# A decode attention and MLP kernel: score and PV matmuls of 32 columns, PV in slices, and weights in other slots

## The chip, the cores and the metric

One core of one Trainium2 chip. The metric is the time on the device in microseconds (us). All runs told here were of the fast state (none over 1.5% above the quickest of the same kernel), each experiment was timed in the same rounds as the kernel before, and ratios are to that kernel. TensorE does the matmuls ("PV" below is the product of the softmax weights with V), VectorE and ScalarE copy and do the softmax, SyncE requests the transfers.

## The reference

Two layers of single-token attention over a long cache, each followed by an MLP block, for two sequences. Cut to what matters:

```python
# B, Sq, D = 2, 1, 576;  H, Sk, Dh = 32, 16384, 128;  F = 4608;  all bf16
def _A_ref(x, k_cache, v_cache, wq, wo):
    q = (x @ wq).reshape(B, Sq, H, Dh).transpose(0, 2, 1, 3)
    scores = jnp.einsum("bhqd,bhkd->bhqk", q, k_cache) * (Dh ** -0.5)
    p = _softmax(scores, axis=-1)
    o = jnp.einsum("bhqk,bhkd->bhqd", p, v_cache)
    return o.transpose(0, 2, 1, 3).reshape(B, Sq, H * Dh) @ wo

def _B_ref(x, w1, w2, w3, w4):          # with S = 1 the shifted parts of h vanish,
    ...                                 # so w1 and w2 add nothing to the result
    x1 = x + hs
    return x1 + _gelu(_layernorm(x1) @ w3) @ w4

x = A_x
for _ in range(2):
    x = x + _A_ref(_layernorm(x), A_k_cache, A_v_cache, A_wq, A_wo)
    x = x + _B_ref(_layernorm(x), B_w1, B_w2, B_w3, B_w4)
```

The K and V caches are read once per layer: 64 (sequence, head) pairs of 4.19 MB of K and 4.19 MB of V, twice. With the weights that is 1122 MB, far more than anything else the kernel does.

## The kernel before

A "head" below is one such pair: 16384 cache rows, that is 128 blocks of 128 rows for K and as many for V. K and V each have five slots in on-chip memory; a slot takes half a head (64 blocks, 2.097 MB), so a head needs four transfers. All are requested by SyncE, in order.

TensorE works in groups of 8 blocks: it transposes 8 K blocks into PSUM, VectorE or ScalarE copies them into `ktbuf`, and two groups later TensorE multiplies them by q, one column each:

```python
for gi, (u, gu, go) in enumerate(groups):          # 16 groups of a head
    if gi + LA < n_g:
        emit_transposes(*groups[gi + LA])          # LA = 2 groups ahead
    ...
    emit_evac(go)                                  # copy tps -> ktbuf, VectorE or ScalarE
    ...
    skey = emit_scores(i, u, gu, go, extra)
    if i >= 1:                                     # small softmax steps of the head before
        if gi == 3:    chain_stage2(hg - 1)
        elif gi == 7:  chain_stage3(hg - 1)
        elif gi == 11: chain_stage4(hg - 1)
state["go"] += n_g
chain_stage1(hg, skey)
if i >= 1:
    emit_pv(i - 1, hg - 1)                         # all 128 PV matmuls of the head before
```

```python
def emit_scores(i, u, gu, go, extra_waits):
    ...
    qcol = qT_sb[:, 2 * h + b:2 * h + b + 1]
    for jj in range(GRP):                          # GRP = 8
        ...
        pe.matmul(sps[:, pb, col:col + 1], ktbuf[:, w, jj * P128:(jj + 1) * P128], qcol, ...)

def emit_pv(i, hg):
    ...
    for half in range(NU):
        P.wait_dma("pe", sd_v[slot], vtot)
        for j in range(UB):                        # UB = 64
            pe.matmul(ops[:, col:col + 1], vslot(slot)[:, j * DH:(j + 1) * DH],
                      pbuf[:, pb, c:c + 1], start=fm, stop=lm)
```

The cache block is the stationary operand in both, so every matmul has its own weight load (16384 of each in both groups of the page). Each K request waits until the last transposes of its slot, each V request until the slot's PV matmuls:

```python
if gu == GPU - 1:                                  # in emit_transposes
    state["kslot_last_t"][slot] = (("tp", e), cnt)
    issue_k_upto(u + NSK)
```

The weights have no room of their own: `wq` and `w4` lie in V slots, `wo` and `w3` in K slots, and they wait until those are free:

```python
wq_sb = vreg[:, 0:DC * H * DH].rearrange("p (c n) -> p c n", c=DC)
wo_sb = kreg[:, 0:H * D].rearrange("p (h n) -> p h n", h=H)
...
if (not first) and u < NSK:
    waits.append(("m1", state["mlp1"]))            # K of layer 2 waits for the w3 product
...
load_wo([t for t in state["kslot_last_t"] if t is not None])   # after the last head
emit_pv(NH - 1, hg0 + NH - 1)
```

## Time and profile before

| | before |
|---|---|
| median of the first 3 runs | 2894.87 us (2872.96 to 2900.3) |
| span of the profiled run, mean granted clock | 2885.2 us, 0.753 |
| TensorE matmul and weight load busy | 83% and 79% |
| transfers | 1122.16 MB, 389 GB/s, 93.6% busy |

How such views are read. In the page's slices a digit is a tenth, and PEclk is the TensorE clock that was granted. In a stretch the columns are its bounds and length, the busy time of TensorE matmul, TensorE weight load, VectorE, ScalarE and GpSimd, then granted clock, DMA share and GB/s. A row of a group has busy time and mean length of one instruction in ns, then the idle time before them and what ended it. Matmul lengths are modelled and overlap; the distance between starts is the better measure of what one costs.

The page of the kernel before: the chain of work that ended last by engine, three groups of TensorE, and the loads of a K or V slot with their time to landing.

```profile
PE 72%; DVE 11%; issue 8%; DMA 5%; ACT 2%; SPq 2%; DVEq 0%; ACTq 0%
...
L415 PE MATMUL tps<-ident,kreg 128*128 128x128 bf16 x16384 | 1604.8, 257 | 57.6 <-issue 44.0
...
L451 PE MATMUL sps<-qT_sb,ktbuf 128*128 128x1 bf16 x16384 | 751.1, 167 | 253.6 <-DVE ktbuf L432 183.6
...
L539 PE MATMUL ops<-pbuf,vreg 128*128 128x1 bf16 x16384 | 449.0, 164 | 92.5 <-issue 86.2
...
kreg<-in_A_k_cache_dram SPq DMA_DIRECT2D x256, 2048.0 KB, 10.7
vreg<-in_A_v_cache_dram SPq DMA_DIRECT2D x256, 2048.0 KB, 17.6
```

The chain runs through TensorE for 72% of the span and through a transfer for 5%, although the transfers are 93.6% busy. The PV matmuls (L539) hardly wait for V: their idle time is "issue", time with no releaser. The scores (L451) wait for the copies of the transposed blocks.

### The profile page before, as it was taken

What the parts mean: (1) busy time and instruction counts of PE and PEld (TensorE: products, weight loads), DVE (VectorE), ACT (ScalarE), POOL (GpSimd) and SP (SyncE); (2) the same over time, 40 slices, a digit from 0 to 9 for tenths busy, and PEclk for the clock granted to TensorE, in tenths of its full rate; (3) what the DMA queues carried; (4) which work ended last, traced back from release to release, by engine and by line L of the source; (5) the groups of instructions that cost most, each with busy time, mean ns of one, the idle gap of its engine ahead of it and who ended that gap; (6) DMA issues with size and microseconds to landing.
All of it is one profiled execution on the core that took longest, in us unless ns stands there. A gap on an engine that the chain in (4) does not pass through costs nothing.

```text
span 2885.2 us, 108634 instructions
## 1 busy us (share of the span) xinstructions
PE 2396.5 (83%) x50814; PEld 2273.3 (79%) x50814; DVE 1121.5 (39%) x2626; ACT 787.8 (27%) x1084; POOL 1.3 (0%) x9
## 2 busy tenths in 40 slices
PE   6888898888888888887568887888988889888885
PEld 6788888888888788887357887888878788878883
DVE  3343433344443444334134434443343444334441
ACT  2222222223222223222023222222222322223220
POOL 0000000000000000000000000000000000000000
PEclk9777765688876887668678758877687886777776
DMA  9999999999999999998879999999999999999985
GB/s 393 414 375 421 401 388 378 376 413 416 422 409 378 403 410 425 402 381 350 309 294 425 414 380 396 410 404 407 406 391 397 421 417 391 400 374 402 408 342 214
DMA packets 95593, 1122.16 MB, mean 389 GB/s; under 512 B 8740, under 2 KB 27304, under 8 KB 27304
## 3 DMA queue, kind: packets, MB, share of 16 engines
q1 hardware_dynamic: 95144, 1115.22, 93.6%
q8 instruction: 399, 6.54, 0.9%
q14 instruction: 50, 0.41, 0.0%
HBM read 1115.18 MB, written 0.00 MB: 387 GB/s over the span
## 4 chain that ended last, share of the span: by engine, by line
PE 72%; DVE 11%; issue 8%; DMA 5%; ACT 2%; SPq 2%; DVEq 0%; ACTq 0%
PE tps L415 37%; PE sps L451 15%; PE ops L539 14%; DVE ktbuf L432 7%; DMA vreg<-in_A_v_cache_dram 2%; SPq L634 2%; PE xps L487 2%; ACT ktbuf L434 1%; PE xps L502 1%; DVE stat L477 1%; PE xps L475 1%; ACT stat L492 1%; DMA vreg<-in_A_wq_dram 1%; DVE stat L490 1%; DVE stat L505 1%
## 5 line engine op out<-in xcount | busy, mean ns | idle before, releaser
L415 PE MATMUL tps<-ident,kreg 128*128 128x128 bf16 x16384 | 1604.8, 257 | 57.6 <-issue 44.0
L415 PEld LDWEIGHTS tps<-ident,kreg 128*128 128x128 bf16 x16384 | 1232.7, 116 | 72.4 <-issue 49.6
L432 DVE COPY ktbuf<-tps 128x1024 bf16<-128x1024 bf16 x1366 | 903.3, 687 | 656.6 <-PE tps L415 654.8
L434 ACT ACTIVATE ktbuf<-tps 128x1024 bf16<-128x1024 bf16 x682 | 695.3, 1019 | 1283.6 <-PE tps L415 1280.9
L451 PE MATMUL sps<-qT_sb,ktbuf 128*128 128x1 bf16 x16384 | 751.1, 167 | 253.6 <-DVE ktbuf L432 183.6
L451 PEld LDWEIGHTS sps<-qT_sb,ktbuf 128*128 128x128 bf16 x16384 | 698.1, 104 | 323.3 <-DVE ktbuf L432 244.7
L539 PE MATMUL ops<-pbuf,vreg 128*128 128x1 bf16 x16384 | 449.0, 164 | 92.5 <-issue 86.2
L539 PEld LDWEIGHTS ops<-pbuf,vreg 128*128 128x128 bf16 x16384 | 434.8, 99 | 96.1 <-issue 89.2
L477 DVE TENSOR_REDUCE stat<-xps 1x1 f32<-1x128 f32 x128 | 35.7, 279 | 322.6 <-PE xps L475 322.6
L465 ACT ACTIVATE ebuf<-sps,stat 128x128 bf16<-128x128 f32 x128 | 47.0, 367 | 338.8 <-DVE stat L463 338.8
L492 ACT ACTIVATE stat<-stat 128x1 f32<-128x1 f32 x128 | 37.7, 295 | 340.4 <-DVE stat L490 340.4
L505 DVE RECIPROCAL stat<-xps 128x1 f32<-128x1 f32 x128 | 21.5, 168 | 214.6 <-PE xps L502 214.6
L490 DVE COPY stat<-xps 128x1 f32<-128x1 f32 x128 | 20.2, 158 | 194.3 <-PE xps L487 194.3
L461 DVE TENSOR_REDUCE stat<-sps 128x1 f32<-128x128 f32 x128 | 37.3, 291 | 142.8 <-PE sps L451 142.8
L487 PE MATMUL xps<-stat,ones 1*128 1x1 f32 x256 | 54.1, 278 | 1.1 <-DVE stat L479 1.1
L502 PE MATMUL xps<-stat,ones 128*128 128x1 f32 x256 | 52.9, 276 | 1.5 <-DVE stat L495 1.5
L487 PEld LDWEIGHTS xps<-stat,ones 1*128 1x128 f32 x256 | 43.1, 210 | 4.0 <-DVE stat L479 1.7
L502 PEld LDWEIGHTS xps<-stat,ones 128*128 128x128 f32 x256 | 44.8, 220 | 1.7 <-DVE stat L495 1.7
L475 PE MATMUL xps<-identf,stat 128*1 128x128 f32 x128 | 42.8, 334 | 1.2 <-issue 1.2
L495 DVE TENSOR_TENSOR stat<-stat 128x1 f32<-128x1 f32 x128 | 20.4, 159 | 46.3 <-ACT stat L492 46.3
L647 PE MATMUL aps<-yT_sb,kreg 128*128 128x2 bf16 (+1 forms) x360 | 22.7, 173 | 17.6 <-DMA kreg<-in_B_w_dram 17.6
L647 PEld LDWEIGHTS aps<-yT_sb,kreg 128*128 128x128 bf16 (+1 forms) x360 | 20.5, 106 | 19.8 <-DMA kreg<-in_B_w_dram 17.8
(68 smaller groups left out, 280.2 us busy)
## 6 DMA issues: line engine op xcount, KB each, us to landing
kreg<-in_A_k_cache_dram SPq DMA_DIRECT2D x256, 2048.0 KB, 10.7
vreg<-in_A_v_cache_dram SPq DMA_DIRECT2D x256, 2048.0 KB, 17.6
vreg<-in_B_w_dram SPq DMA_DIRECT2D x2, 5184.0 KB, 29.2
kreg<-in_A_wo_dram SPq DMA_DIRECT2D x2, 4608.0 KB, 15.6
kreg<-in_B_w_dram SPq DMA_DIRECT2D x8, 1152.0 KB, 8.7
vreg<-in_A_wq_dram SPq DMA_DIRECT2D x8, 1024.0 KB, 12.2
kreg<-in_B_w_dram SPq DMA_DIRECT2D x2, 576.0 KB, 14.8
vreg<-in_B_w_dram SPq DMA_DIRECT2D x8, 144.0 KB, 6.4
```

What stands on the lines that cost most here:

```text
L415: cnt = P.emit("pe", lambda pe, t=t, jj=jj, j=j, slot=slot: pe.transpose(tps[:, t, jj * P128:(jj + 1) * P128], kslot(slot)[:, j * DH:(j + ...
L432: fn = lambda E, w=w, t=t: E.tensor_copy(ktbuf[:, w, :], tps[:, t, :])
L434: fn = lambda E, w=w, t=t: E.activation(ktbuf[:, w, :], tps[:, t, :], AF.Copy)
L451: cnt = P.emit("pe", lambda pe, pb=pb, col=col, w=w, jj=jj, qcol=qcol: pe.matmul(sps[:, pb, col:col + 1], ktbuf[:, w, jj * P128:(jj + 1) * ...
L475: ch["tm"] = P.emit("pe", lambda pe: pe.transpose(xps[0:1, 0:P128], st[:, 0:1], identf[:, :]), waits=[("mx", ch["mx"])], signal="tm")
L477: ch["Mr"] = P.emit("dve", lambda d: d.tensor_reduce(s1[0:1, 0:1], xps[0:1, 0:P128], AX.X, ALU.max), waits=[("tm", ch["tm"])], signal="Mr")
L487: ch["bc"] = P.emit("pe", lambda pe: pe.matmul(xps[:, P128:P128 + 1], ones[0:1, 0:P128], s1[0:1, 1:2], start=True, stop=True), waits=[("nM ...
L492: ch["wp"] = P.emit("act", lambda a: a.activation(st[:, 4:5], st[:, 0:1], AF.Exp, bias=st[:, 3:4], scale=SCALE), waits=[("cp", ch["cp"])], ...
L502: ch["tot"] = P.emit("pe", lambda pe: pe.matmul(xps[:, P128 + 1:P128 + 2], ones[:, :], st[:, 5:6], start=True, stop=True), waits=[("tq", c ...
L505: c = P.emit("dve", lambda d: d.reciprocal(st[:, 7:8], xps[:, P128 + 1:P128 + 2]), waits=[("tot", ch["tot"])], signal="d3")
L539: pe.matmul(ops[:, col:col + 1], vslot(slot)[:, j * DH:(j + 1) * DH], pbuf[:, pb, c:c + 1], start=fm, stop=lm),
L634: P.dma("sp", lambda sp, c=c, r0=r0, r1=r1: sp.dma_start(w1_chunk(c)[0:r1 - r0, :], B_w1[r0:r1, :]), sd_w1)
```

## The change

Three things in one. The scores and PV matmuls stream 32 columns where one is needed, the other 31 being ignored, to keep the array active. PV is cut into slices of 8 that run with each group, one head later than before, which needs four softmax buffers. The weights go to K and V slots that come free early, so that transfers go on between the layers. The core of the diff, with cuts marked:

```diff
+NPB = 4
+NW = 32
...
-            qcol = qT_sb[:, 2 * h + b:2 * h + b + 1]
+            qc = 2 * h + b
+            qcols = qT_sb[:, qc:qc + NW]
...
-                    sps[:, pb, col:col + 1], ktbuf[:, w, jj * P128:(jj + 1) * P128], qcol, start=True, stop=True),
+                    sps[:, sb, col:col + NW], ktbuf[:, w, jj * P128:(jj + 1) * P128], qcols, start=True, stop=True),
...
+        def emit_pv_slice(i, hg, nblk):
+            pb = hg % NPB
+            col = i
...
+            for c in range(j0, j1):
...
+                cnt = P.emit("pe", lambda pe, col=col, slot=slot, j=j, c=c, pb=pb, fm=first_mm, lm=last_mm:
+                             pe.matmul(ops[:, col:col + NW], vslot(slot)[:, j * DH:(j + 1) * DH],
+                                       pbuf[:, pb, c:c + NW], start=fm, stop=lm),
...
                 skey = emit_scores(i, u, gu, go, extra)
+                if i >= 2:
+                    emit_pv_slice(i - 2, hg - 2, pv_per_group)
+                    if last and pvstate[hg - 2] == UB:
+                        issue_v_upto(NUNITS - 1)
+                        load_wo(lay, [state["kslot_last_t"][WO_SLOT[lay]], state["kslot_last_t"][WO_SLOT[lay] + 1]])
...
-            if i >= 1:
-                emit_pv(i - 1, hg - 1)
-        issue_v_upto(NUNITS - 1)
-        load_wo([t for t in state["kslot_last_t"] if t is not None])
...
+    WO_SLOT = (3, 2)
+    W3_AT = ((0, F, 2 * F, 3 * F, 4 * F), (0, F, 2 * F, 4 * UNIT_ELEMS, 2 * UNIT_ELEMS))
+    WQ_AT = tuple(3 * UNIT_ELEMS + c * H * DH for c in range(DC - 1)) + (2 * UNIT_ELEMS,)
...
-                waits.append(("m1", state["mlp1"]))
+                waits.append(("pj", state["proj"]) if s >= 3 else ("m1", state["mlp1"]))
...
         if not first:
-            load_wq([("m2", state["mlp2"])])
+            load_wq([("pv", state["last_pv"])], list(range(DC - 1)))
+            issue_k_upto(2)
+            load_wq([("m2", state["mlp2"])], [DC - 1])
...
+        for c in range(DC - lay):
+            load_w3(c, w3_waits if c == 0 else ())
...
+        if lay == 1:
+            load_w3(DC - 1, [("pj", state["proj"])])
```

The junk columns of a matmul are overwritten by the next matmuls, which is why PV now writes column i, heads in order, and not 2h+b.

## The prediction

> **What bounds the kernel now.** I read the page's engine rows and slices first, then the waits, then stretches of 20 us, then one head instruction by instruction.
>
> ```profile
> PE 2396.5 (83%) x50814; PEld 2273.3 (79%) x50814; DVE 1121.5 (39%) x2626; ACT 787.8 (27%) x1084; POOL 1.3 (0%) x9
> ...
> PEclk9777765688876887668678758877687886777776
> DMA  9999999999999999998879999999999999999985
> GB/s 393 414 375 421 401 388 378 376 413 416 422 409 378 403 410 425 402 381 350 309 294 425 414 380 396 410 404 407 406 391 397 421 417 391 400 374 402 408 342 214
> ```
>
> Two things are nearly full: TensorE and the transfers. The GB/s row is the telling one. It reaches 425 and falls to about 375 wherever the TensorE clock row is low (seventh and eighth slices). A pure transfer bound would not do that. The stretches of 20 us say it more sharply (last three columns: granted clock, DMA share, GB/s):
>
> ```profile
> 340.00:360.00 20.00, 18.68 (x264) 17.80 (x262) 7.02 (x16) 5.30 (x6) 0.00 (x0) 0.50 0.90 367
> ...
> 600.00:620.00 20.00, 15.46 (x368) 14.82 (x365) 8.48 (x20) 5.75 (x8) 0.00 (x0) 0.83 1.01 428
> ...
> 1380.00:1400.00 20.00, 14.04 (x194) 7.87 (x194) 3.96 (x13) 1.04 (x2) 0.00 (x0) 0.74 0.38 133
> ...
> 2820.00:2840.00 20.00, 11.80 (x105) 5.21 (x102) 3.72 (x11) 0.20 (x1) 0.00 (x0) 0.73 0.34 117
> ```
>
> Over the 129 steady stretches (60 to 1360 and 1500 to 2780 us) the mean is clock 0.755 and 402 GB/s. The 22 of them at clock 0.60 or less average 371 GB/s, the 72 at 0.80 or more 413, and the 59 with DMA share 1.00 or more 423. So about 424 GB/s is what the transfers give when always fed, and TensorE's slow spells starve them: a K load waits until a slot's transposes are done (the DMA queue's own waits on those transposes sum to 2408 us). The last two lines are the ends of the two attention layers, where transfers stand still.
>
> Why TensorE is slow, in one head (start, length, engine; then 1 us stretches):
>
> ```profile
> 507.26 0.46 PEld L415 LDWEIGHTS tps<-ident,kreg 128*128 128x128 bf16 x8
> ...
> 507.67 0.30 PEld L451 LDWEIGHTS sps<-qT_sb,ktbuf 128*128 128x128 bf16 x8
> ...
> 507.90 0.46 PEld L415 LDWEIGHTS tps<-ident,kreg 128*128 128x128 bf16 x8
> ...
> 513.08 3.57 PE L539 MATMUL ops<-pbuf,vreg 128*128 128x1 bf16 x128
> ...
> 520.37 0.22 PE L451 MATMUL sps<-qT_sb,ktbuf 128*128 128x1 bf16 x3 [2.78 <-issue]
> ...
> 521.49 0.77 PEld L415 LDWEIGHTS tps<-ident,kreg 128*128 128x128 bf16 x8
> ...
> 522.56 0.77 PEld L415 LDWEIGHTS tps<-ident,kreg 128*128 128x128 bf16 x8
> ```
>
> ```profile
> 515.00:516.00 1.00, 1.00 (x46) 1.00 (x44) 0.00 (x0) 0.14 (x1) 0.00 (x0) 1.00 1.08 442
> 516.00:517.00 1.00, 1.00 (x32) 1.00 (x30) 0.00 (x0) 0.00 (x0) 0.00 (x0) 0.79 0.92 377
> 517.00:518.00 1.00, 0.60 (x10) 0.54 (x9) 0.48 (x1) 0.00 (x0) 0.00 (x0) 0.50 0.98 401
> ```
>
> A group of 8 transposes and 8 scores takes 0.64 us at clock 1.00 (507.26 to 507.90) and 1.07 at 0.50 (521.49 to 522.56). The burst of 128 one-column PV matmuls (3.57 us, 27 ns each) ends with the clock falling to 0.50 and then a 2.78 us hole with no releaser. The burst is what costs the clock.
>
> [...]
>
> **The change part by part.**
>
> *32 columns in scores and PV* (2 x 16384 matmuls). [...]I put the added time at zero[...]. What they add is array activity[...]. That should bring the full clock back[...], where today the half clock sometimes lasts a whole head (340 to 360).
>
> *PV sliced, 8 per group, one head later, with four softmax buffers.* It removes the burst and spreads the instructions evenly. TensorE per head at full clock: 16 x (0.64 + 8 x 0.027) = 13.7, plus about 0.8 for the five small fp32 matmuls: 14.5 us. At half clock: 16 x (1.07 + 0.22) + 0.8 = 21.4 us. Stalls today: 163 us of "issue" before transposes, scores and PV (44.0 + 33.1 + 86.2) and 219 us of scores waiting for VectorE or ScalarE copies (183.6 + 35.1), 382 / 128 = 3.0 us a head. Check on today: half the time cold gives about 14.5 + 0.45 x 6.9 + 3.0 = 20.6 us against the observed 8.44 MB / 402 = 21.0 us. Afterwards the PV slice lengthens the time between a transpose group and its scores from 0.64 to 0.86 us, so the copies are hidden better[...]; I allow 1 us of stalls and a quarter of groups cold: 14.5 + 1.7 + 1 = 17.2 us.
>
> The transfers of a head (4 x 2.097 MB at 424 GB/s) take 19.8 us. So TensorE gets 2.6 us to spare and the transfers bind. Does the new lag starve them? V of head i-1 is requested near the end of head i-1 and needed at the start of head i+1; when TensorE waits there, two K and two V loads are already queued behind it. They stay fed. I leave 10 us of the steady loss, which today is the sum over the 129 stretches of 20 us x (1 - GB/s / 424) = 131 us.
>
> *Weights in slots that free early.* Between the layers (1360 to 1500) the same sum gives 52 us lost. Now the output weight is loaded during the last head, w3 needs only the transposes done, and wq (four of five chunks), K and w4 no longer stand behind the MLP. From the start t0 of the last head I get: last V landed at 20, output weight 32, w3 46, w4 60, w1 and wq 72, K up to 98; TensorE: PV done 24, projection 33 to 43 (10 us as today), norms 8, w3 product 11, w4 product 12, then wq product to 98, first scores 99, next K request about 103. Transfers idle 5 us; the short rows of w4 and the output weight (302 GB/s today: 4.7 MB in 15.6) cost another 7: 12 us.
>
> *The end.* Today 50 us lost. The last chunk of w3 now sits behind w4 and w1 in the queue (landed at 62), so the w3 product starts no earlier than the queue allows, and the chain from there (11 + 2 + 12 + 4 = 29 us) has no transfers left; with short rows 36 us. This part gains little. The start costs 5 us as today.
>
> Sum: 1122.2 MB / 424 = 2647, + 5 + 12 + 36 + 10 = 2710 us. [...]
>
> **The rivals.** (a) *The wider matmuls are not free*: [...]TensorE needs 20.6: the steady part stays where it is and only the ends are gained, about 2840 us. For it: weight load and matmul might not overlap for short streams. Against: 8 transposes take 0.41 us (507.26 to 507.67), 51 ns each[...]. (b) *The clock falls elsewhere*: TensorE, now ahead, waits up to 5 us for V at a head's start[...], and starts each head cold. This is self-limiting: a cold start uses up the wait. If half of each head ran cold, 14.5 + 3.5 + 1 = 19 us, still under 19.8, and some 20 to 40 us are lost: 2740. (c) *Nothing gained in the steady part*, the transfers being the bound already (DMA row of nines): only the ends count, 54 us, 2840. Against it the 371 versus 413 GB/s.
>
> **Range and chances.** The floor is 1122 MB at 427 GB/s plus the ends, about 2665. Rival (b) plus a longer boundary gives 2775. Both (a) and (c) end near the 2% line (2837 us). Predicted 2710 us, 8 in 10 between 2665 and 2775; faster by over 2% 0.95, within 2% 0.04, slower 0.01.
>
> **What would show it.** Right: steady GB/s near 420 in all slices, PEclk mostly 9, transposes waiting for K or PV for V instead of "issue", V landing later than today's 17.6 us (queued behind others), a PV matmul still at 27 ns spacing, a DMA row with no dent between the layers but one at the end. Wrong: matmul spacing of 40 ns at 32 columns; a clock still near 0.75 with GB/s at 400; or a dent of 40 us left at mid-span.

It is an estimate that 32 columns add no time and bring the full clock back, and so are the quarter of groups cold and the 1 us of stalls behind the 17.2 us. For rival (a) the step to 20.6 us is 3.4 us more a head; the trace gives about as much: if each of the 256 matmuls took a quarter of the 51 ns of a transpose besides, it would be 3.3 us a head, and TensorE would need 20.5 (an estimate). The argument against (a) rested on more than the 51 ns that are left of it; that the weight load is hidden was not shown there. That short rows are what made the output weight land at 302 GB/s (4.7 MB in 15.6 us) was not shown either. The 427 GB/s of the range is within what the fullest stretches show (428 from 600 to 620 us).

## The result

| | before | after |
|---|---|---|
| median | 2886.8 us (2871.52 to 2912.22, 15 runs) | 2741.28 us (2739.31 to 2742.9, 12 runs) |
| ratio | 1 | 0.9487, 95% interval 0.946 to 0.9514 |
| span of the profiled run, granted clock | 2885.2 us, 0.753 | 2740.1 us, 0.933 |
| TensorE matmul busy | 83% | 78% |
| transfers busy, GB/s | 93.6%, 389 | 97.7%, 410 |

A ratio here is the mean time of one kernel's runs over the mean of the other's in the same rounds, so it is not quite the ratio of the medians quoted.

The page of the kernel after, the lines that answer to those of before:

```profile
PEclk9999999999999999999789999999999999999997
DMA  9999999999999999999989999999999999999995
GB/s 393 426 419 423 423 417 418 415 417 425 419 415 419 418 422 420 419 413 403 375 341 424 426 420 417 409 425 424 419 420 407 424 425 420 416 416 416 424 401 209
...
PE 45%; DMA 37%; DVE 8%; issue 5%; ACT 3%; SPq 2%; DVEq 0%; ACTq 0%
...
L441 PE MATMUL tps<-ident,kreg 128*128 128x128 bf16 x16384 | 1329.7, 226 | 54.2 <-issue 40.2
...
L478 PE MATMUL sps<-qT_sb,ktbuf 128*128 128x32 bf16 x16384 | 756.0, 179 | 361.2 <-DVE ktbuf L458 235.0
...
L578 PE MATMUL ops<-pbuf,vreg 128*128 128x32 bf16 x16384 | 728.9, 178 | 131.8 <-DMA vreg<-in_A_v_cache_dram 87.6
...
kreg<-in_A_k_cache_dram SPq DMA_DIRECT2D x256, 2048.0 KB, 16.7
vreg<-in_A_v_cache_dram SPq DMA_DIRECT2D x256, 2048.0 KB, 20.7
```

The clock row is nines but for the time between the layers and the end. The valleys of 375 to 380 GB/s inside the layers are gone. The chain has moved from TensorE to the transfers (5% to 37%), and the PV matmuls now wait mostly for V (87.6 us) and less for "issue" (43.4 us, where it was 86.2). Loads land later, K after 16.7 us where it was 10.7, as they would if they queue behind each other.

One head of the kernel after, the weight loads of TensorE in order of time (start, length). First at full clock, then, after the first cut, where the clock is half:

```profile
500.92 0.45 PEld L441 LDWEIGHTS tps<-ident,kreg 128*128 128x128 bf16 x8
501.33 0.30 PEld L478 LDWEIGHTS sps<-qT_sb,ktbuf 128*128 128x128 bf16 x8
501.57 0.27 PEld L578 LDWEIGHTS ops<-pbuf,vreg 128*128 128x128 bf16 x8
501.77 0.46 PEld L441 LDWEIGHTS tps<-ident,kreg 128*128 128x128 bf16 x8
...
516.25 0.77 PEld L441 LDWEIGHTS tps<-ident,kreg 128*128 128x128 bf16 x8
...
517.54 0.77 PEld L441 LDWEIGHTS tps<-ident,kreg 128*128 128x128 bf16 x8
```

A group is 0.85 us at full clock (500.92 to 501.77): 8 transposes in 0.41, 8 scores in 0.24, 8 PV in 0.20. So a pair of weight load and 32-column matmul costs 25 to 30 ns, what one column cost in the kernel before (27 ns in its PV burst, 29 in the 8 scores from 507.67 to 507.90). At half clock a group is 1.29 us (516.25 to 517.54). The half clock comes for one spell of about 3.6 us (an estimate) in some half of the heads: of the 122 steady stretches of 20 us (a head each, nearly), 52 show a mean clock of 0.91, and 0.09 x 20 / 0.5 is 3.6; 54 show 1.00, and nine show 0.83 to 0.86, about two such spells.

Where the time went, by the prediction's own measure (the sum over stretches of 20 us x (1 - GB/s / 424), with the steady part of after taken from 60 to 1280 and 1420 to 2640 us):

| lost against 424 GB/s, us | before | predicted | after |
|---|---|---|---|
| floor, 1122.2 MB at 424 | 2647 | 2647 | 2647 |
| start | 5 | 5 | 5 |
| steady | 131 | 10 | 25 |
| between the layers | 52 | 12 | 25 |
| end | 50 | 36 | 38 |
| sum | 2885 | 2710 | 2740 |

The two ends of after. First a stretch between the layers and one at the end, then the two records of TensorE that explain them (start, length; in brackets, the idle time before and what ended it):

```profile
1380.00:1400.00 20.00, 16.17 (x257) 15.20 (x258) 3.59 (x6) 1.04 (x2) 0.00 (x0) 0.52 0.54 204
...
2700.00:2720.00 20.00, 7.92 (x125) 7.15 (x125) 0.42 (x6) 0.58 (x1) 0.00 (x0) 0.50 0.45 143
```

```profile
1383.51 10.10 PE L362 MATMUL aps<-yT_sb,vreg 128*128 128x2 bf16 x160 [7.20 <-DMA vreg<-in_A_wq_dram]
...
2712.49 11.35 PE L709 MATMUL aps<-yT_sb,kreg 128*128 128x2 bf16 x180 [12.02 <-DMA kreg<-in_B_w_dram]
```

Between the layers the q product waits 7.20 us for the last chunk of `wq`, which is requested late. At the end the w3 product waits 12.02 us for the last chunk of `w3`, which is requested behind `w4` and `w1`. Both are repaired in an experiment below.

### The profile page after: what moved, and what is told of

Same layout as the page of the kernel before. It is cut to its first block, busy times and chain, and to the rows that moved or that the text cites. A ratio compares the mean times of both kernels' runs of the same rounds, so it can differ in the third digit from the quotient of the medians.

```text
span 2740.1 us, 108636 instructions
## 1 busy us (share of the span) xinstructions
PE 2139.2 (78%) x50814; PEld 1991.5 (73%) x50814; DVE 1114.2 (41%) x2628; ACT 783.5 (29%) x1084; POOL 2.0 (0%) x11
## 3 DMA queue, kind: packets, MB, share of 16 engines
q1 hardware_dynamic: 95176, 1115.22, 97.7%
q8 instruction: 399, 6.54, 0.9%
## 4 chain that ended last, share of the span: by engine, by line
PE 45%; DMA 37%; DVE 8%; issue 5%; ACT 3%; SPq 2%; DVEq 0%; ACTq 0%
DMA vreg<-in_A_v_cache_dram 35%; PE tps L441 19%; PE sps L478 11%; PE ops L578 10%; DVE ktbuf L458 5%; ACT ktbuf L460 2%; PE xps L515 1%; PE aps L709 1%; SPq L694 1%; PE xps L530 1%; PE aps L362 1%; PE xps L734 1%; SPq L403 1%; DMA kreg<-in_A_k_cache_dram 1%; ACT stat L520 1%
## 5 line engine op out<-in xcount | busy, mean ns | idle before, releaser
L441 PE MATMUL tps<-ident,kreg 128*128 128x128 bf16 x16384 | 1329.7, 226 | 54.2 <-issue 40.2
L441 PEld LDWEIGHTS tps<-ident,kreg 128*128 128x128 bf16 x16384 | 1015.0, 101 | 69.1 <-issue 49.5
L478 PE MATMUL sps<-qT_sb,ktbuf 128*128 128x32 bf16 x16384 | 756.0, 179 | 361.2 <-DVE ktbuf L458 235.0
L478 PEld LDWEIGHTS sps<-qT_sb,ktbuf 128*128 128x128 bf16 x16384 | 628.9, 98 | 452.0 <-DVE ktbuf L458 304.8
L578 PE MATMUL ops<-pbuf,vreg 128*128 128x32 bf16 x16384 | 728.9, 178 | 131.8 <-DMA vreg<-in_A_v_cache_dram 87.6
L578 PEld LDWEIGHTS ops<-pbuf,vreg 128*128 128x128 bf16 x16384 | 561.7, 97 | 139.6 <-issue 138.0
L537 DVE TENSOR_SCALAR pbuf<-ebuf,stat 128x128 bf16<-128x128 bf16 x128 | 32.5, 254 | 4.8 <-DVE stat L535 0.3
## 6 DMA issues: line engine op xcount, KB each, us to landing
kreg<-in_A_k_cache_dram SPq DMA_DIRECT2D x256, 2048.0 KB, 16.7
```

The lines of the kernel that those rows point to most:

```text
L441: cnt = P.emit("pe", lambda pe, t=t, jj=jj, j=j, slot=slot: pe.transpose(tps[:, t, jj * P128:(jj + 1) * P128], kslot(slot)[:, j * DH:(j + ...
L478: cnt = P.emit("pe", lambda pe, sb=sb, col=col, w=w, jj=jj, qcols=qcols: pe.matmul(sps[:, sb, col:col + NW], ktbuf[:, w, jj * P128:(jj + 1 ...
L578: pe.matmul(ops[:, col:col + NW], vslot(slot)[:, j * DH:(j + 1) * DH], pbuf[:, pb, c:c + NW], start=fm, stop=lm),
```

## The experiments

The theory: TensorE's slow clock kept K slots from coming free, and so starved the transfers; streaming 32 columns brings the clock back, and the slices and the weight placement add little, or only at the ends. Rivals: the slices do it, by removing the burst that the prediction blamed; or the steady part was bound by transfers all along. First each part alone.

### a1_pad_only: the kernel before with 32 columns, and nothing else

```diff
-            qcol = qT_sb[:, 2 * h + b:2 * h + b + 1]
+            qcol = qT_sb[:, 2 * h + b:2 * h + b + NW]
-                    sps[:, pb, col:col + 1], ...
+                    sps[:, pb, col:col + NW], ...
-                                 pe.matmul(ops[:, col:col + 1], ..., pbuf[:, pb, c:c + 1], ...
+                                 pe.matmul(ops[:, col:col + NW], ..., pbuf[:, pb, c:c + NW], ...
```

> The kernel before with 32 columns in scores and PV, nothing else (PV still one burst, weights as before). Theory A, [...]the burst now streams 32 columns per 27 ns, so the clock no longer falls after it; granted clock above 0.88, steady loss from 131 to about 40 us, time about 2795 us; the issue holes stay (about 160 us in all on the tensor engine). Rival B, only the slicing matters[...]: clock stays at 0.75, time 2870 to 2900.

Measured: 2767.41 us beside 2892.14 of before, ratio 0.9552 (0.9517 to 0.9587), clock 0.913. The loss in the steady part (60 to 1280 and 1440 to 2640 us) is 24 us, as small as in the full change, with the burst still there. The holes named "issue" fell from 163 to 103 us, where I had expected them to stay. Half of a burst in its trace, TensorE by time, and the instruction that follows:

```profile
506.13 1.89 PE L542 MATMUL ops<-pbuf,vreg 128*128 128x32 bf16 x64 [2.66 <-DMA vreg<-in_A_v_cache_dram]
507.86 1.01 PE L418 MATMUL tps<-ident,kreg 128*128 128x128 bf16 x8
```

64 matmuls of 32 columns take 1.73 us from start to start, 27 ns each. With one column the burst of the kernel before took 27 ns each too, so here the extra columns cost nothing, and they alone bring most of the gain.

### a2_slice_nopad: the kernel after with one column

```diff
-NW = 32
+NW = 1
```

> The changed kernel with one column instead of 32. Theory A: half-clock spells come back, clock 0.80 or less, steady loss 60 to 100 us, time 2780 to 2830 us. Rival B: as the changed kernel, 2741 us within 10, clock 0.9 or more.

Measured: 3106.11 us, ratio 1.0731 (1.0676 to 1.0786), clock 0.557: slower than before by 7%. My figures were far off, and the slices without the columns turn out to do harm. The clock row of its page:

```profile
PEclk9555555556555555556576556555555555557556
```

The clock stays at half almost throughout, and the steady part (60 to 1440 and 1600 to 3000 us) loses 376 us. The waits named "issue" before transposes, scores and PV are only 9 us together here (163 before), so no hole is needed to keep the clock down. Its weight loads at half clock (start, length):

```profile
1000.88 0.77 PEld L441 LDWEIGHTS tps<-ident,kreg 128*128 128x128 bf16 x8
1001.61 0.42 PEld L478 LDWEIGHTS sps<-qT_sb,ktbuf 128*128 128x128 bf16 x8
1001.95 0.29 PEld L578 LDWEIGHTS ops<-pbuf,vreg 128*128 128x128 bf16 x8
1002.16 0.08 PEld L503 LDWEIGHTS xps<-identf,stat 128*1 128x1 f32 x1
```

A half-clock group with one-column PV is 1.28 us (1000.88 to 1002.16), and its 8 transposes, the only matmuls of more than one column, take 0.73 of that, 57%. In the kernel before a half-clock group is 1.07 us with the same 0.73 for the transposes (521.49 to 522.22), 68%, because the PV matmuls were elsewhere. So spreading one-column matmuls over all groups thinned out the groups, and here the clock hardly comes back (0.557 in the mean, where it was 0.753). That the second follows from the first is my reading; the runs with other numbers of columns, below, try it.

### a3_weights_only: one column and the burst, with the new weight places

```diff
 # the kernel after with NW = 1, and in place of the slices:
+            if i >= 1:
+                emit_pv_all(i - 1, hg - 1)
 # and the last V requests and the output weight are requested at the start of the last head
```

> The changed kernel with the PV burst put back and one column: that is the kernel before with only the weights placed and requested early. Both theories: the steady loss of 131 us stays, the loss between the layers falls by 25 to 30 us and the end by about 12, so about 2845 us, clock 0.75.

Measured: 2845.61 us, ratio 0.9829 (0.9782 to 0.9877), clock 0.758, and a steady loss of 131 us, that of before. This part gains only at the ends, 46 us, as expected.

### a4_burst: the kernel after with 32 columns and the burst put back

The edit is that of a3_weights_only with NW = 32.

> The changed kernel with the PV burst put back, 32 columns kept. If the padding alone keeps the clock (theory A in its strong form) the slicing is worth little: about 2755 us, clock 0.9. If the burst's instruction holes matter (rival B): 2800 us or more with holes of 2 to 3 us after each burst.

Measured: 2745.0 us, ratio 0.9471 (0.9436 to 0.9505), clock 0.921. The kernel after has 0.9487 (0.946 to 0.9514), so what the slices bring cannot be told from nothing. The holes are still there: 198 us named "issue", one of them soon after this burst of 32 columns:

```profile
509.11 3.38 PE L578 MATMUL ops<-pbuf,vreg 128*128 128x32 bf16 x128
...
517.03 0.29 PE L441 MATMUL tps<-ident,kreg 128*128 128x128 bf16 x1 [4.14 <-issue]
```

That is more than the 163 us of before and the 115 of after, and this kernel is as fast as after: with the clock back, such holes cost next to nothing. The parts as a table (medians in us; that of after is from its own rounds):

| | old weight places, burst | new places, burst | new places, slices |
|---|---|---|---|
| 1 column | 2892 (before) | 2846 | 3106 |
| 32 columns | 2767 | 2745 | 2741 (after) |

The columns are worth 101 to 125 us with a burst and 365 with slices. The weight places are worth 46 us alone and 22 beside the columns. The slices do harm with one column and nothing that can be seen with 32.

### b1_nw8, c1_nw16, b2_nw128: the dose

```diff
-NW = 32
+NW = 8        # c1: 16, b2: 128
```

> The changed kernel with 8 columns. Theory: [...]Eight columns give[...] between, clock 0.65 to 0.90, time 2745 to 2950 us. If any padding beyond one column is enough (a count of instructions or of non-trivial matmuls): as 32, 2741 us.

> The changed kernel with 16 columns. [...] Theory[...]: clock between the 0.77 of 8 columns and the 0.93 of 32, about 0.85; the tensor engine still keeps ahead of the transfers in most heads: 2742 to 2775 us. If the clock has a step between 8 and 32 that goes by something else (column count itself): either as 8 (2826 us) or as 32 (2741 us).

> The changed kernel with 128 columns. [...]a head takes [...]21.2 us plus 1 to 2 of waits, over the 19.8 of the transfers: 2860 to 3050 us at clock 0.95 or more, and the tensor engine binds again. If the floor and the streaming add up (rival a of the prediction)[...]: 3700 us or more.

The theory in short: the more columns a half-clock group has, the sooner the full clock comes back. The 21.2 us a head for 128 columns, and the rival's 3700 us, stand as estimates.

Measured:

| columns | granted clock | median us | ratio (95%) |
|---|---|---|---|
| 1 | 0.557 | 3106.11 | 1.0731 (1.0676 to 1.0786) |
| 8 | 0.766 | 2825.6 | 0.9803 (0.9743 to 0.9862) |
| 16 | 0.851 | 2752.2 | 0.9533 (0.9492 to 0.9575) |
| 32 | 0.933 | 2741.28 | 0.9487 (0.946 to 0.9514) |
| 128 | 0.989 (its steady part has no half clock) | 3398.59 | 1.175 (1.1702 to 1.1799) |

The clock rises with the number of columns. With 128 columns the clock is best and the time worst, and worse than I expected. The weight loads of that run in order of time say why:

```profile
1003.31 0.49 PEld L578 LDWEIGHTS ops<-pbuf,vreg 128*128 128x128 bf16 x8
1003.76 0.49 PEld L441 LDWEIGHTS tps<-ident,kreg 128*128 128x128 bf16 x8
...
1004.66 0.49 PEld L578 LDWEIGHTS ops<-pbuf,vreg 128*128 128x128 bf16 x8
```

Eight matmuls of 128 columns take 0.45 us, 56 ns each, and a group 1.35 us. Sixteen groups are 21.6 us, the small matmuls 0.8, the weight loads' waits for copies 3.0 (389 us over 128 heads): 25.4 us a head, against 19.8 for its transfers. The steady part of this run moves 334 GB/s, which is 25.1 us for a head's 8.39 MB. TensorE binds, as I expected, but my 21.2 us and 1 to 2 of waits were too small: the groups and the small matmuls take 22.4, and the waits are 3.0.

### c2_pv_pad and c3_score_pad: 32 columns in one place only, with the burst

```diff
 # a4_burst, with two widths
+NWS = 1       # scores; c3: 32
+NWP = 32      # PV;     c3: 1
```

The question: does the burst's fall of the clock matter, or the return from it? With columns in PV only, the burst has 32 of them and the groups are those of the kernel before. With columns in the scores only, the burst is that of the kernel before and the groups have 32; by the theory the burst still brings the clock down, and the groups win it back.

> Burst order (as a4_burst), 32 columns in PV only, scores one column. The prediction's sentence 'the burst is what costs the clock' says this is enough: [...]clock 0.9, about 2750 us. The later theory says that what matters is how soon the clock comes back, and that needs the columns in the groups of transposes and scores[...]: clock 0.75 to 0.83, 2780 to 2830 us.

> Burst order, 32 columns in the scores only, PV one column. 'The burst costs the clock': the clock falls after every burst as before, 0.75 to 0.8, 2800 us or more. 'The return matters': it falls, but comes back[...]: clock 0.86 to 0.90, 2745 to 2765 us.

Measured: c2 2810.03 us, ratio 0.9724 (0.9685 to 0.9764); c3 2763.3 us, ratio 0.9563 (0.9529 to 0.9598). The clocks are 0.853 and 0.847, so the times went as the theory of the return says, and the clocks did not: I had expected 0.75 to 0.83 for c2 and 0.86 to 0.90 for c3. With a3_weights_only (one column in both, 2846 us) and a4_burst (32 in both, 2745) this is a full square in one order: the columns are worth 83 us in the scores alone, 36 in PV alone, 101 in both. Two neighbouring stretches of c2, then one of c3 that stands for most of its run:

```profile
880.00:900.00 20.00, 17.42 (x328) 16.74 (x326) 7.57 (x18) 5.75 (x8) 0.00 (x0) 0.62 0.84 340
900.00:920.00 20.00, 17.88 (x283) 17.00 (x283) 7.56 (x19) 4.33 (x6) 0.00 (x0) 0.57 0.79 318
```

```profile
400.00:420.00 20.00, 17.09 (x389) 16.47 (x388) 7.80 (x20) 6.52 (x9) 0.00 (x0) 0.83 1.00 418
```

In c3 the clock falls in nearly every head and returns soon: 90 of its 122 stretches from 60 to 1280 and 1420 to 2640 us have a clock between 0.6 and 0.9 and average 416 GB/s, none is at 0.6 or less. In c2 it falls less often, but can stay down for much of two heads: of the same 122, 4 at 0.6 or less average 338 GB/s, and 51 between average 398. So with nearly one mean clock (c1, c2 and c3 have 0.847 to 0.853) the times are 2752, 2810 and 2763 us. In these runs short cold spells are taken up by the five slots (416 GB/s in c3's stretches between 0.6 and 0.9), long ones are not (338 in c2's four at 0.6 or less); the mean clock alone does not tell the time. The "issue" holes before transposes, scores and PV do not explain c2's loss: it has 201 us of them, but c3 has 183, and a4_burst, which differs from c2 only in the scores' columns, has 198 and is 65 us faster.

### b3_floor: how far down the transfers go

One of 8 scores and one of 8 PV matmuls, all transposes, copies and transfers kept. This computes the wrong thing on purpose. The comparison with the reference for this kernel says little about the attention sum.

```diff
 ...
-            for jj in range(GRP):                 # in emit_scores
+            for jj in range(1):
 ...
-            for c in range(j0, j1):               # in emit_pv_slice
+            for c in range(j0, j1, 8):
 ...
```

> The changed kernel with one of eight score matmuls and one of eight PV matmuls (wrong result on purpose; loads, transposes, copies and softmax stay). If the transfers bind the steady part, as the prediction has it, taking half of the tensor engine's work away gains only the remaining steady loss and some of the ends: 2705 to 2730 us. If the tensor engine still binds in part: below 2690 us.

Measured: 2697.23 us, ratio 0.9325 (0.9286 to 0.9363), a little below the range that I had put. TensorE is busy for 58% of the span and its clock is 0.815, yet the steady part (60 to 1280 and 1420 to 2600 us) moves 426 GB/s. The wait of its PV matmuls, from the waits (us in total, times, longest):

```profile
PE ops L578 <- DMA vreg<-in_A_v_cache_dram: 663.6, 127, 7.3
```

TensorE waits for V 127 times in 128 heads. So the transfers bind here. The kernel after stands 44 us above this run, but not all of that is to be had: without most of its matmuls this run also fetches fewer instructions, 2.87 MB where the kernel after fetches 6.54. The difference is about 9 us at 424 GB/s, so the floor of this layout is nearer 2706 us (an estimate).

### b4_better: the two late chunks requested earlier

The last chunk of `wq` goes into `ktbuf`, which is free between the layers, and is requested with the other four. The last chunk of layer 2's `w3` goes into V slot 3 and is requested before `w4`.

```diff
+        if c == DC - 1:                           # wq_cols
+            return wqx[:, n0:n1]                  # a view of ktbuf
+        if lay == 1 and c == DC - 1:              # w3_chunk
+            return vreg[:, 3 * UNIT_ELEMS:3 * UNIT_ELEMS + F]
 ...
-            load_wq([("pv", state["last_pv"])], list(range(DC - 1)))
-            issue_k_upto(2)
-            load_wq([("m2", state["mlp2"])], [DC - 1])
+            load_wq([("pv", state["last_pv"])], list(range(DC)))
 ...
-        for c in range(DC - lay):
-            load_w3(c, w3_waits if c == 0 else ())
+        for c in range(DC):
+            load_w3(c, w3_waits if c == 0 else [("pv", state["vslot_last_pv"][3])] if lay == 1 and c == DC - 1 else ())
 ...
-        if lay == 1:
-            load_w3(DC - 1, [("pj", state["proj"])])
```

> The changed kernel with two more weight chunks moved: the last chunk of w3 of the second layer goes into a V slot that is free after the last head but one and is requested before w4; the last chunk of wq goes into the idle transposed-K buffer and is requested with the other four. If the ends are chains as read in the profile after: the 12.0 us wait of the w3 product at the end and the 7.2 us wait of the q product between the layers vanish, 2741 - 17 = about 2724 us. Rival: the transfers are only reordered and the next wait takes over (w4 at the end, K between the layers): less than 6 us gained.

Measured: 2722.77 us (2722.09 to 2725.84), ratio 0.9415 (0.9384 to 0.9447), clock 0.937. The start of the w3 product at the end, as TensorE's record has it:

```profile
2691.94 0.24 PE L711 MATMUL aps<-yT_sb,kreg 128*128 128x2 bf16 x4 [0.60 <-DVE yT_sb L345]
```

The 12.02 us wait for `w3` is gone: the product waits 0.60 us, for its other operand. By the same measure the loss between the layers went from 25 to 16 us and at the end from 38 to 29, which is close to the 18.5 us between the two medians. This version beats both kernels.

### d1_better64: that kernel with 64 columns

```diff
-NW = 32
+NW = 64
```

> The rearranged kernel (2722.8 us, clock 0.937, in its run) with 64 columns instead of 32. [...]a group keeps its 0.85 us[...]. [...]the clock rises to 0.97 or more. Rival, that this last fall comes from waits for data[...]: the clock stays near 0.937 and[...] the time rises. As to time: if the last cold windows still starve the transfers, a risen clock gives 2700 to 2712; if the five slots absorb them already (as the kernels with the same clock and different times suggest) the time stays within 2715 to 2727 even with the risen clock.

The theory was that more columns end the cold spells that are left.

Measured: 2725.71 us (2723.48 to 2727.83), ratio 0.945 (0.9416 to 0.9484), clock 0.977. In its steady part the clock is 0.990 and the "issue" holes of the run are 68 us, and still it moves 419.6 GB/s, what the kernel after moves at clock 0.946. So removing the last cold spells in this way gains nothing. (A group is 0.92 us here, not the 0.85 that I had put down: about 1.1 us a head, more than the 0.7 that the cold spells of the kernel after cost it, as an estimate. So this run does not show what a faster TensorE would gain.)

What is left shows in one of its slow stretches, 560 to 580, at clock 1.00 and 394 GB/s. First SyncE's requests (start, and time until the last of them was out), then two stretches of 1 us:

```profile
556.43 10.93 SPq L395 DMA_DIRECT2D kreg<-in_A_k_cache_dram  x2
567.40 0.91 SPq L409 DMA_DIRECT2D vreg<-in_A_v_cache_dram  x2
```

```profile
565.00:566.00 1.00, 1.00 (x27) 1.00 (x28) 0.53 (x1) 0.00 (x0) 0.00 (x0) 1.00 1.03 442
...
567.00:568.00 1.00, 1.00 (x33) 1.00 (x30) 0.00 (x0) 0.96 (x1) 0.00 (x0) 1.00 0.53 213
```

From 545.50 to 556.43 one K, two V and again one K slot were requested, 19.8 us of transfers at 424 GB/s, so if nothing older was queued they last until about 565. The next K request stood until 567, and the two V requests stood behind it, in order. The transfers ran low for some 4 us. This is one place, read and not tested: a version that asks for V before a K that has to wait is what I would try next.

## Why the prediction was right, and where its sum was not

**32 columns cost nothing: right.** 27 ns in a1_pad_only's burst, 25 to 30 in the kernel after, where one column took 27 to 29. Rival (a) is refuted.

**They bring the full clock back: right, and it is the whole gain of the steady part.** a1_pad_only alone takes the steady loss from 131 to 24 us, with the clock at 0.913, and the dose runs show the clock rising with the columns, from 0.557 at 1 to 0.933 at 32.

**"The burst is what costs the clock": half right.** A burst of one-column PV does set off a fall (in c3_score_pad nearly every head has one, at a clock of 0.847; with PV padded as well, in a4_burst, the clock is 0.921). What made it expensive was that the groups of transposes and scores did not win the clock back soon: c2_pv_pad, with 32 columns in its burst, takes 2810 us, c3_score_pad, with 32 in its groups, 2763. The 2.78 us hole that the prediction saw after the burst is not the cost either: a4_burst has more of such holes and is as fast as the kernel after. Cutting up the burst without the columns, which by this step should have helped, made the kernel 7% slower.

**TensorE at 17.2 us a head, with 1 us of stalls: too good.** The group was right (0.85 us, where 0.86 was put). But the scores' waits for copies did not shrink: they went from 219 us to 327 (235.0 behind VectorE, 92.4 behind ScalarE), which fits that a copy takes as long as before (686 ns on VectorE) while TensorE is faster. With 115 us of "issue" that is 442 / 128 = 3.5 us a head. The cold spells were less than the quarter allowed: a steady clock of 0.946 is 11% of the time, 2.1 us a head, of which 1 - 0.85 / 1.29 is lost, 0.7 us. As an estimate 14.5 + 0.7 + 3.5 = 18.7 us, still under 19.8, so the conclusion held: the transfers bind, with 1.1 us to spare and not 2.6.

**Steady loss 10 us: measured 25, the first mis-sized term.** It has two parts, counted on the 122 stretches. In the 104 with a DMA share of 1.00 or more the rate is 422.2 GB/s and not 424, which makes 9 us. The other 18 average 404.5, which makes 17. b3_floor moves 426, so 422 is not the transfers' own limit; what takes the last per cent is not settled (b3_floor's instruction fetches take 0.4% of the transfer engines' time, those of the kernel after 0.9%, which may be a part). The dips do not need the half clock: d1_better64 has one at clock 1.00, where the order of requests is a cause that was read in one place. TensorE's time probably has a share in them, for b3_floor, with an eighth of its score and PV matmuls, has no steady stretch under 413 GB/s.

**Between the layers 12 us: measured 25, the second.** The step that failed is the timeline in which `wq` (landed at 72) no longer holds up the q product. Its last chunk held it up by 7.20 us, and the one stretch from 1380 to 1400 lost 10.4 us (20 x (1 - 204 / 424)), where 5 us of idle transfers had been allowed in all. b4_better removed that wait and 9 us of the loss. The four stretches from 1300 to 1380 lost 10 us more with the transfer engines busy (share 0.97 to 1.07), where 7 had been put for short rows (that the rows' length is the cause was not tested).

**End 36 us: measured 38.** As put, the last chunk of `w3` behind `w4` and `w1` sets it. b4_better shows that placement could have gained more: it loses 29 us.

The sum, 2647 + 5 + 25 + 25 + 38, is 2740 us; the two mis-sized terms are 28 of the 30 us missing. Of the rivals, (b) occurs in a mild form: the half clock is 11% of the steady time, not half of each head, and d1_better64 won nothing back by removing it. That the measured 2741 us is the 2740 put for (b) is chance. (c) is refuted: the steady rate went from 402 to 420 GB/s. Two slips of the working change nothing: the check on today took 0.45 of the time as cold where clock 0.755 means 0.49 (20.9 us), and the "22 at clock 0.60 or less" are 23 as displayed (370 GB/s).

Open: why the holes named "issue" appear (they are few where TensorE is slow, 9 us in a2_slice_nopad against 163 before, but no run tested a cause); and what keeps the steady rate at 422 and not 426.

## What to carry to other kernels

Measure what a small matmul costs from start to start: where more columns cost nothing, columns that nobody reads can bring the clock back. Here one of 32 columns cost 25 to 30 ns and one of a single column 27 to 29, and with 31 columns that nobody reads in each the granted clock was 0.933 where it was 0.557 without. Spreading thin matmuls evenly among good ones can be worse than a burst (here 3106 us against 2846), and a mean clock does not tell the time (2752, 2763 and 2810 us at 0.847 to 0.853): ask how long the longest cold spell is against the buffers ahead. Once the transfers bind, look at what stands behind a waiting request in the queue (in one place here the transfers fell to 213 GB/s while two V requests had stood behind a K request).
